# An RWKV channel mix between attention and MLP: another reckoning for the planned order, x loaded by pairs, one activation table, an earlier weight load

## The chip, the cores and the metric

The kernel runs on one core of a Trainium2 chip. The metric is the device time of one execution in microseconds (us); lower is better. TensorE is written PE, its weight loads PEld, VectorE DVE, ScalarE ACT, GpSimd POOL; SP is the engine that issues nearly all DMAs.

## The reference

```python
def _attn_ref(u, v, z):                      # u, v: (4, 3072, 256); z: (4, 3072, 64)
    scores = np.matmul(z, z.transpose(0, 2, 1)) / S
    attn = np.maximum(scores, 0.0) ** 2
    return u * np.matmul(attn, v)

def _moe_ref(x, mu_k, mu_r, w_k, w_v, w_r):  # w_k: (256, 1024), w_v: (1024, 256), w_r: (256, 256)
    x_prev = np.concatenate([np.zeros((B, 1, D)), x[:, :-1, :]], axis=1)
    xk = mu_k * x + (1.0 - mu_k) * x_prev
    xr = mu_r * x + (1.0 - mu_r) * x_prev
    k = np.maximum(xk @ w_k, 0.0)
    v = k * k @ w_v
    return v / (1.0 + np.exp(-(xr @ w_r)))

def _moe2_ref(x, w_in, w_out):               # w_in: (256, 2048), w_out: (2048, 256)
    h = np.maximum(x @ w_in, 0.0)
    return (h * h) @ w_out
```

The three run one after the other; the third takes all 4 x 3072 = 12288 rows of the second as one batch. The weights come as float64.

## The kernel before

Matmuls are done in a float32 form of reduced precision, on operands split into a high part (a cast) and a low part (what is left, a subtraction on DVE). A product is the sum of three matmuls of 128x128 by 128x512: high by high, low by high, high by low. A block is 512 of the 12288 rows; there are 24 blocks, and two make a pair.

*Attention* (function `attention`, from line 261) runs over blocks and, in each, over 24 chunks of keys. Steps that aren't part of the product (loads of z, u and v, transposes, conversion of weights from 64-bit form) hang on numbered steps. At its very start SP and ACT each issue halves of the first two loads of z (`load_z`), seven warm-up matmuls run (L584), and PE transposes z (`prep_z`, L292). Its result u * o is stored transposed to DRAM as xT (L478), and loaded from there by the mix as x (`load_x`, L174).

*The mix* has one pair without and eleven with a Strassen-like scheme (function `mix_groups`, line 989 on). The first pair is plain: two gates (12 matmuls each), 16 hidden tiles (6 matmuls each, `plain_hidden`) and their down products (6 each, `plain_down`, lines 236 to 241). A hidden tile takes a relu (L1080) and a square (L1083) on ACT, a cast (L90) on ACT or DVE, and the rest (L1091) on DVE. After that come groups (s, i): pair s, four groups i each, with seven products (`product`, L850), eight down products (L866 to L868), sums of banks on DVE (`add`, L882), relu, square, cast and rest (L887, L891, L90, L899), and the gates (`gate_unit`, `gate_out`, L637). The sums of w_k that this scheme needs are made at the beginning (`load_wk`, `wk_sums`, L659). Beside all this the next pair is prepared: x is scaled on ACT (`scale_x`, L183) and blended on DVE (`blend`, L192), once for the keys, into a tile of the pair `x2`, and once for the gate. Before, `x` has a tile of one block, so a pair's blocks are loaded in turn: the odd one, the even one, and the odd one again for the gate. Nine pieces of MLP weights are converted from 64-bit form (`conversion`, L132 to L156), and four pieces are split for the MLP (`piece_nodes`).

*The order of the mix* is planned when the program is built. Each step is a node with its engine ("P", "V", "S", "D" for a load, "SV" for a cast that ACT or DVE may do), a cost in us, what it depends on and a due time. PE's order is as written. Due times go back from PE's: each node is due when the node that needs it is due, less cost and 0.2. Then a list scheduler runs from time zero: it takes the engine that can start first, and on it the ready node that is due first. The resulting order is written into the engines' queues; each engine then works through its queue in order, waiting for semaphores. The planned times themselves set nothing else. Before, each load costs 3.5 us, and is taken to start when the plan says so:

```python
            def load(f, *a, deps=()):
                return node("D", 3.5, lambda e: f(*a), *deps)
...
            free = {"P": 0.0, "V": 1.0, "S": 1.0, "D": 0.0}
...
                    i = min((i for i, t in cand.items() if t <= start), key=lambda i: (nodes[i][4], i))
```

Small rings of tiles (`held_by`: "a", "t", "h" and three "raw" tiles for loads of 512 KB) are given out by the planner too.

*The MLP* (line 1408 on, order written by hand) has twelve pairs with eight groups each, of the same seven and eight products, with w_in and w_out split piece by piece; the first piece that isn't split during the mix, number 4, is loaded by `second_pools` (L834), which is called behind the mix. In the group after the first, ACT casts that piece (L647).

A load issued by SP or ACT stands in that engine's queue in program order; when it waits for a semaphore, what stands behind it on the queue waits too. A table for ACT's functions is loaded where the program needs one (ACT_TABLE_LOAD): before the first copy (L297) and before the first sigmoid (L637).

## Time and profile before

| | |
|---|---|
| median of the runs of before | 2473.99 us (2473.72 to 2474.18) |
| the profiled execution | 2473.61 us |
| its span | 2471.7 us |
| PE busy | 2456.2 us (99%) |
| PEld busy | 2028.0 us (82%) |
| DVE busy | 2105.1 us (85%) |
| ACT busy | 1815.6 us (73%) |

Attention takes from 0 to 918.7 us of the span, the mix to about 1492, the MLP the rest. The time of the profiled execution and its span differ by 1.9 us, which lie outside of the span. Matmuls overlap, and their ends are modelled; a busy PE of 99% therefore doesn't say that no time is lost there. In the rows further down, idle time ahead of an instruction and what ended it stand in square brackets, and "xN" merges N instructions in a row.

### The profile page before, as it was taken

How to read it: one execution, taken by the hardware profiler on the slowest of the kernel's cores; microseconds unless marked ns; L12 is line 12 of the kernel's file. 1: busy time of each engine (PE TensorE's matmuls, PEld its weight loads, DVE VectorE, ACT ScalarE, POOL GpSimd, SP SyncE). 2: the span in 40 equal slices, each digit the busy share in tenths (PEclk: the TensorE clock that was granted, in tenths of full speed). 3: DMA queues.
4: the chain of work that ended last, by engine and by line, in shares of the span. 5: the costliest groups of instructions: out<-in, count | busy, mean ns of one | idle time of the engine just before them, and what ended most of it. 6: DMA issues, size and time to landing. Idle time of an engine off the chain costs nothing.

```text
span 2471.7 us, 39362 instructions
## 1 busy us (share of the span) xinstructions
PE 2456.2 (99%) x14721; PEld 2028.0 (82%) x14721; DVE 2105.1 (85%) x3520; ACT 1815.6 (73%) x3216; POOL 0.7 (0%) x6
## 2 busy tenths in 40 slices
PE   9999999999999999999999999999999999999999
PEld 7888898888888887888888887888888888888887
DVE  8898999889899979999999898777777777777776
ACT  8867977888688657888887877666666666666665
POOL 0000000000000000000000000000000000000000
PEclk9999999999999999999999999999999999999999
DMA  7677767776866752222211111110011001100100
GB/s 209 188 227 188 206 200 191 212 207 185 228 194 188 209 154 88 94 86 82 69 52 69 54 67 52 35 33 20 18 35 35 18 18 35 35 18 18 35 18 18
DMA packets 309439, 252.16 MB, mean 102 GB/s; under 512 B 205312, under 2 KB 224768, under 8 KB 306176
## 3 DMA queue, kind: packets, MB, share of 16 engines
q1 hardware_dynamic: 307136, 249.13, 34.5%
q8 instruction: 115, 1.88, 0.3%
q10 hardware_dynamic: 2112, 0.52, 0.1%
q14 instruction: 76, 0.62, 0.1%
HBM read 143.69 MB, written 105.91 MB: 101 GB/s over the span
## 4 chain that ended last, share of the span: by engine, by line
PE 86%; DVE 6%; ACT 4%; issue 2%; DMA 1%; DVEq 0%; SPq 0%
PE v L459 27%; PE ups L850 25%; PE v L868 9%; PE v L866 9%; PE v L867 9%; PE sps L421 4%; PE ups L219 2%; ACT a L382 1%; ACT a L425 1%; DVE st L882 1%; DMA x<-xT 1%; DVE hlo L899 1%; DVE alo L435 0%; DVE turn L362 0%; ACT vhl L328 0%
## 5 line engine op out<-in xcount | busy, mean ns | idle before, releaser
L459 PE MATMUL v<-ahi,vhl 64*128 64x512 f32 x4592 | 668.6, 387 | 0.0
L459 PEld LDWEIGHTS v<-ahi,vhl 64*128 64x128 f32 x4592 | 468.5, 184 | 87.5 <-ACT rest L469 3.9
L887 ACT ACTIVATE s<-s 128x512 f32<-128x512 f32 x288 | 181.0, 628 | 319.9 <-DVE s L882 319.9
L459 PE MATMUL v<-alo,vhl 64*128 64x512 f32 x2296 | 410.7, 386 | 0.1
L866 PE MATMUL v<-hhi,wout 128*128 128x512 f32 x768 | 298.9, 389 | 0.6 <-ACT hhi L90 0.6
L868 PE MATMUL v<-hlo,wout 128*128 128x512 f32 x768 | 298.9, 389 | 0.0
L867 PE MATMUL v<-hhi,wout 128*128 128x512 f32 x768 | 298.8, 389 | 0.0
L850 PE MATMUL ups<-d,win 128*128 128x512 f32 x1056 | 296.5, 389 | 0.0
L459 PEld LDWEIGHTS v<-alo,vhl 64*128 64x128 f32 x2296 | 251.4, 184 | 42.7 <-DVE alo L435 0.6
L899 DVE TENSOR_TENSOR hlo<-s,hhi 128x512 fp32r<-128x512 f32 x384 | 264.3, 688 | 18.1 <-ACT hhi L90 2.8
L891 ACT ACTIVATE s<-s 128x512 f32<-128x512 f32 x384 | 231.4, 628 | 6.1
L882 DVE TENSOR_TENSOR s<-ups,su 128x512 f32<-128x512 f32 x192 | 131.3, 684 | 122.0 <-PE ups L850 121.8
L850 PEld LDWEIGHTS ups<-d,win 128*128 128x128 f32 x1056 | 198.2, 188 | 41.2
L850 PE MATMUL ups<-b,win 128*128 128x512 f32 x792 | 222.4, 389 | 0.0
L435 DVE TENSOR_TENSOR alo<-a,ahi 128x512 fp32r<-128x512 f32 x334 | 219.3, 660 | 0.0
L425 ACT ACTIVATE a<-a 128x512 f32<-128x512 f32 x334 | 211.4, 633 | 10.3
L362 DVE STREAM_TRANSPOSE turn<-a 128x512 f32<-128x512 f32 x240 | 206.5, 860 | 13.9 <-ACT a L425 12.3
L382 ACT ACTIVATE a<-sps 128x512 f32<-128x512 f32 x335 | 197.5, 590 | 19.7 <-PE sps L421 17.1
L850 PEld LDWEIGHTS ups<-b,win 128*128 128x128 f32 x792 | 148.7, 188 | 30.9
L866 PEld LDWEIGHTS v<-hhi,wout 128*128 128x128 f32 x768 | 144.1, 188 | 31.6 <-ACT hhi L90 1.0
L868 PEld LDWEIGHTS v<-hlo,wout 128*128 128x128 f32 x768 | 144.1, 188 | 30.4 <-DVE hlo L899 0.4
L867 PEld LDWEIGHTS v<-hhi,wout 128*128 128x128 f32 x768 | 144.1, 188 | 29.5
(199 smaller groups left out, 4265.4 us busy)
## 6 DMA issues: line engine op xcount, KB each, us to landing
turned<-turn SPq DMA_DIRECT2D x60, 1024.0 KB, 5.0
mixed<-turned SPq DMA_DIRECT2D x220, 256.0 KB, 5.1
x<-xT SPq DMA_DIRECT2D x31, 513.0 KB, 3.8
u<-in_u_dram SPq DMA_DIRECT2D x192, 64.0 KB, 3.6
xT<-uT SPq DMA_DIRECT2D x48, 256.0 KB, 2.4
x2d<-sig SPq DMA_DIRECT2D x48, 256.0 KB, 2.0
x<-x2d SPq DMA_DIRECT2D x12, 1024.0 KB, 4.7
out_dram<-y SPq DMA_DIRECT2D x94, 128.0 KB, 2.3
```

Of the source, the lines that this page charges most:

```text
L362: nc.vector.transpose(t[:, :, :, c, :], a.rearrange("x (m r q) -> x q m r" if s else "x (m q r) -> x q m r", m=G, q=R))
L382: nc.scalar.activation(out=a, in_=ps, func=AF.Relu, scale=1.0 / S)
L425: nc.scalar.activation(out=a, in_=a, func=AF.Square)
L435: finish(lambda: nc.vector.tensor_tensor(out=lo, in0=a, in1=hi, op=ALU.subtract))
L459: nc.tensor.matmul(acc[n, d][i], lhsT=vt[rows, k % 2, c, ds_], rhs=at[s][k // 2][rows], start=first and k == 0, stop=last and k == 2)
L850: nc.tensor.matmul(ps, lhsT=weight(g, h, w), rhs=ops[g[0], j][y], start=first and m == 0, stop=m == 2, skip_group_check=not first)
L866: nc.tensor.matmul(acc[p, b][d], lhsT=w[:, 0, c, ds_], rhs=hi, start=first, stop=False)
L867: nc.tensor.matmul(acc[p, b][d], lhsT=w[:, 1, c, ds_], rhs=hi, start=False, stop=False)
L868: nc.tensor.matmul(acc[p, b][d], lhsT=w[:, 0, c, ds_], rhs=lo, start=False, stop=last)
L887: nc.scalar.activation(out=tmp[g, c], in_=banks[g, 0] if c == "11" else tmp[g, c], func=AF.Relu, scale=1.0 if g[0] < NPAIR else HS)
L891: nc.scalar.activation(out=tmp[g, c], in_=tmp[g, c], func=AF.Square)
L899: nc.vector.tensor_tensor(out=lo, in0=tmp.pop((g, c)), in1=hi, op=ALU.subtract)
```

## The change

- A sigmoid of one column on ACT stands ahead of the first loads of z, into a place that is written again later.
- x of a pair is loaded at once (`load_pair`), into the pair's tile `x2`, which gets eight more columns ahead of each of its two channel halves; the last of them holds the row before the pair. Scaling (`before_x`) reads it shifted by one, and the blend (`blend_x`) is done in place; the first half's blend also waits for the second half's scaling. The load waits until the operands of the pair before are made. The gate's x is still loaded by blocks, after the gate operand before it.
- Loads cost 4.5 (a pair's 5.5) in the plan; the conversions and the sums of w_k can't be planned before `late`, 12 us, plus 1.0.
- In the plan's head, three hidden tiles come before the first gate on PE.
- The costs in the plan are multiplied by a margin (1.05 on DVE, 1.06 on ACT), DVE and ACT are free from 4.0, PE's lag is 0.2, and a cast that ACT may do too counts as due 9 us later when DVE chooses.
- Piece 4 is loaded by a node of the plan, after the last conversion and the last piece before it, into the third raw tile; `second_pools` no longer loads it.

```diff
@@ -573,6 +573,7 @@
                 for i in range(ND * (2 - n)):
                     at_step(s - 1 + 12 * n + 2 * i, mix, n, i // ND, i % ND)
             ones = nc.const_aps.tensor(1.0, [P, T], BF16)
+            nc.scalar.activation(out=om[:, 0, 0:1], in_=ones[:, 0:1], func=AF.Sigmoid)
             load_z(0, 0, (nc.sync, nc.scalar))
             nc.sync.dma_start(out=v_first, in_=v[0, 0:T, :].rearrange("(c p) d -> p c d", p=P))
             load_z(0, 1, (nc.scalar, nc.sync))
@@ -715,19 +716,38 @@
 
     unit = {}
 
-    def staged_x(s, b, c):
-        if s not in x2_raw:
-            x2_raw[s] = hp.tile([P, ND, 2 * T], F32, tag="x2", name="x2")
-        return x2_raw[s][:, c, b * T:(b + 1) * T]
-
-    def stage_x(s, b, c, m=None):
-        blend(2 * s + b, 0, c, staged_x(s, b, c), m)
+    HALO = 8
+
+    def pair_tile(s):
+        x2_raw[s] = hp.tile([P, ND, HALO + 2 * T], F32, tag="x2", name="x2")
+        return x2_raw[s]
+
+    def pair_x(s):
+        return x2_raw[s][:, :, HALO:].rearrange("x c (b t) -> x c b t", b=2)
+
+    def load_pair(s):
+        b, t0 = 2 * s // NB, 2 * s % NB * T
+        t = pair_tile(s)
+        src = xT[b].rearrange("(c p) s -> p c s", p=P)
+        if t0:
+            nc.sync.dma_start(out=t[:, :, HALO - 1:], in_=src[:, :, t0 - 1:t0 + 2 * T])
+        else:
+            nc.vector.memset(t[:, :, HALO - 1:HALO], 0.0)
+            nc.sync.dma_start(out=t[:, :, HALO:], in_=src[:, :, 0:2 * T])
+
+    def before_x(s, b, c, m):
+        t0 = HALO - 1 + b * T
+        nc.scalar.activation(out=m, in_=x2_raw[s][:, c, t0:t0 + T], func=AF.Copy, scale=om[:, 0, c:c + 1])
+
+    def blend_x(s, b, c, m):
+        x = pair_x(s)[:, c, b]
+        nc.vector.scalar_tensor_tensor(out=x, in0=x, scalar=mu[:, 0, c:c + 1], in1=m, op0=ALU.mult, op1=ALU.add)
...
     def op_src(s, j):
-        src = x2_raw[s].rearrange("x c (b t) -> x c b t", b=2)
+        src = pair_x(s)
         if j in (2, 3):
             return x2_tmp[s][:, j - 2]
         return src[:, *{0: (0, 0), 1: (0, 1), 4: (1, 0), 5: (1, 1), 6: (1, 0)}[j]]
@@ -802,11 +822,11 @@
         next(splits[i])
 
     def load_x2(s):
-        x2_raw[s] = t = hp.tile([P, ND, 2 * T], F32, tag="x2", name="x2")
-        nc.sync.dma_start(out=t, in_=x2d[s - NPAIR].rearrange("(c p) t -> p c t", p=P))
+        t = pair_tile(s)
+        nc.sync.dma_start(out=t[:, :, HALO:], in_=x2d[s - NPAIR].rearrange("(c p) t -> p c t", p=P))
 
     def prep_x2(s, k):
-        src = x2_raw[s].rearrange("x c (b t) -> x c b t", b=2)
+        src = pair_x(s)
         b11, b12, b21, b22 = src[:, 0, 0], src[:, 0, 1], src[:, 1, 0], src[:, 1, 1]
         if k == 0:
             x2_tmp[s] = t = hp.tile([P, 2, T], F32, tag="d13", name="d13")
@@ -817,11 +837,13 @@
             nc.vector.tensor_tensor(out=b21, in0=b21, in1=b12, op=ALU.subtract)
         else:
...
             return halves(t[:, 0], t[:, 1], x)
 
@@ -831,7 +853,6 @@
         pools["ops", 1] = ctx.enter_context(tc.tile_pool(name="ops1", bufs=1, side="right", reuse_waits="tile"))
         for q in range(2, 4):
             w_tiles(w4, q)
-        load_piece(4)
 
     def mlp():
         gt, acc = {}, {}
@@ -1018,8 +1039,8 @@
             def on_pe(f, *a, deps=(), cost=0.68):
                 return node("P", cost, lambda e: f(*a), *deps)
 
-            def load(f, *a, deps=()):
-                return node("D", 3.5, lambda e: f(*a), *deps)
+            def load(f, *a, deps=(), cost=4.5):
+                return node("D", cost, lambda e: f(*a), *deps)
 
             def get(*k):
                 return last.get(k)
@@ -1030,18 +1051,15 @@
                 last["op", s, j] = on_v(op_lo, s, j, deps=(hi,))
                 return last["op", s, j]
 
-            def blended(n, which, c, *deps):
-                place = (lambda: raw_r(n, c)) if which else (lambda: staged_x(n // 2, n % 2, c))
-                m = on_s(lambda: scale_x(n, which, c, place()), deps=(*deps, get("x", n)), cost=0.63)
-                if which:
-                    take(m, "t", ("xr", n, c))
-                f = (lambda: blend_r(n, c, place())) if which else (lambda: stage_x(n // 2, n % 2, c, place()))
-                return on_v(f, deps=(m,), cost=0.63)
+            def gate_blend(n, c, *deps):
+                m = on_s(lambda: scale_x(n, 1, c, raw_r(n, c)), deps=(*deps, get("x", n)), cost=0.63)
+                take(m, "t", ("xr", n, c))
+                return on_v(lambda: blend_r(n, c, raw_r(n, c)), deps=(m,), cost=0.665)
 
             def gate_operand(n, *deps):
                 done = []
                 for c in range(ND):
-                    xm = use(blended(n, 1, c, *deps), ("xr", n, c))
+                    xm = use(gate_blend(n, c, *deps), ("xr", n, c))
                     hi = use(either(r_hi, n, c, deps=(xm,)), ("xr", n, c))
                     last["xr", n, c] = use(on_v(r_lo, n, c, deps=(hi,)), ("xr", n, c))
                     done.append(xm)
@@ -1108,13 +1126,19 @@
                     cast(on_act, hi, xr1[c])
 
             def prepare(s, clear):
-                m0 = 2 * s
-                last["x", m0 + 1] = load(load_x, m0 + 1, deps=last["xr done"])
-                b1 = [blended(m0 + 1, 0, c, *clear) for c in range(ND)]
-                last["x", m0] = load(load_x, m0, deps=b1)
-                b0 = [blended(m0, 0, c, *clear) for c in range(ND)]
-                last["staged", s] = [*b0, *b1]
-                last["b0"] = b0
+                ready = load(load_pair, s, deps=clear, cost=5.5)
+                done, m_of = [], {}
+                for b in (1, 0):
+                    for c in range(ND):
+                        def scaled(b=b, c=c):
+                            m_of[b, c] = place.pop(("m", s, b, c))
+                            before_x(s, b, c, m_of[b, c])
+                        m = take(on_s(scaled, deps=(ready,), cost=0.63), "t", ("m", s, b, c))
+                        f = lambda b=b, c=c: blend_x(s, b, c, m_of[b, c])
+                        done.append((b, c, m, f))
+                m1 = {c: m for b, c, m, f in done if b}
+                xs = [use(on_v(f, deps=(m, None if b else m1[c]), cost=0.665), ("m", s, b, c)) for b, c, m, f in done]
+                last["staged", s] = xs
                 head(s)
 
             def head(s):
@@ -1124,16 +1148,19 @@
                 operand(s, 1, on_v(sums, s, 1, deps=(last["tops"],)))
 
             def gate_part(s, r_free):
-                xs = gate_operand(2 * s, *r_free)
-                last["x", 2 * s + 1] = load(load_x, 2 * s + 1, deps=(*xs, *last["b0"]))
+                last["x", 2 * s] = load(load_x, 2 * s, deps=last["xr done"])
+                last["x", 2 * s + 1] = load(load_x, 2 * s + 1, deps=gate_operand(2 * s, *r_free))
 
             def tail(s):
                 for j in range(2, 6):
                     operand(s, j, last["tops"])
                 operand(s, 6, on_v(sums, s, 2, deps=(last["op", s, 4], last["op", s, 1])))
 
+            late = node("D", 12.0, lambda e: None)
+
             def wk_nodes(h, *deps):
                 total = use(take(load(load_wk, h, deps=(get("wk"),)), "raw", ("wk32", h)), ("wk32", h))
+                total = node("D", 1.0, lambda e: None, total, late)
                 for k in range(2):
                     total = use(on_v(wk_sums, h, k, deps=(total,), cost=0.7), ("wk32", h))
                     if k == 0:
@@ -1146,6 +1173,7 @@
             def conversion(i, src, put, due):
                 key = "w", i
                 i = use(take(load(load_raw, key, src, src.shape[1], src.shape[2], deps=(last.get("conv"),)), "raw", key), key)
+                i = node("D", 1.0, lambda e: None, i, late)
                 steps = convert(key, put, 0)
                 for k, f in enumerate(steps):
                     i = on_v(f, deps=(i,), cost=0.6 if k in (3, 6, 7) else 0.335, due=due)
@@ -1186,6 +1214,8 @@
                 use(on_pe(down1, n, f, False, cost=0.91, deps=(hi,)), ("h", n, f))
                 return use(on_pe(down1, n, f, True, cost=0.45, deps=(lo,)), ("h", n, f))
 
+            for k in order1[:lead]:
+                plain_hidden(*k)
             plain_gate(0)
             for c in range(ND):
                 m = take(on_s(plain_m, c, deps=(last["r", 0],), cost=0.63), "a", ("xr1", c))
@@ -1195,8 +1225,6 @@
                 for i in (xm, hi, last["xr", 1, c]):
                     use(i, ("xr1", c))
                 last.setdefault("xr done", []).append(xm)
-            for k in order1[:lead]:
-                plain_hidden(*k)
             prepare(PLAIN, ())
             for i, (n, f) in enumerate(order1):
                 if i + lead < len(order1):
@@ -1333,8 +1361,12 @@
                     piece_nodes(PIECE_PAIRS.index(s), 49.0 + 46.2 * s)
                 before = g
 
+            take(load(load_piece, 4, deps=(last["piece"], last["conv"])), "raw", ("w32", 4))
+
             n = len(nodes)
-            LAG = {"P": 0.3, "V": 0.15, "S": 0.15, "D": 0.0}
+            MARGIN = {"P": 1.0, "V": 1.05, "S": 1.06, "D": 1.0}
+            BEHIND_CASTS = 9.0
+            LAG = {"P": 0.2, "V": 0.15, "S": 0.15, "D": 0.0}
 
             def cost_on(i, e):
                 c = nodes[i][1]
@@ -1348,7 +1380,7 @@
             for i in reversed(range(n)):
                 for d in nodes[i][3]:
                     nodes[d][4] = min(nodes[d][4], nodes[i][4] - cost_on(i, nodes[i][0][0]) * (nodes[i][0] != "P") - 0.2)
-            free = {"P": 0.0, "V": 1.0, "S": 1.0, "D": 0.0}
+            free = {"P": 0.0, "V": 4.0, "S": 4.0, "D": 0.0}
             users, missing = [[] for _ in nodes], [len(x[3]) for x in nodes]
             for i, x in enumerate(nodes):
                 for d in x[3]:
@@ -1361,7 +1393,7 @@
                 t = ready[i]
                 for ring, key in takes.get(i, ()):
                     free_at = [(max([ended[k] + 0.15 for k in users_of[x]], default=0.0), q) for q, x in enumerate(held_by[ring])
-                               if all(k in ended for k in users_of[x])]
+                               if all(k in ended for k in users_of[x]) and (key != ("w32", 4) or q == 2)]
                     if not free_at:
                         return None
                     t, chosen[i] = max(t, min(free_at)[0]), (ring, min(free_at)[1], key)
@@ -1377,7 +1409,7 @@
                     if not cand:
                         continue
                     start = max(free[e], min(cand.values()))
-                    i = min((i for i, t in cand.items() if t <= start), key=lambda i: (nodes[i][4], i))
+                    i = min((i for i, t in cand.items() if t <= start), key=lambda i: (nodes[i][4] + BEHIND_CASTS * (e + nodes[i][0] == "VSV"), i))
                     if best is None or start < best[0]:
                         best = start, e, i
                 start, e, i = best
@@ -1385,8 +1417,9 @@
                     pe.pop(0)
                 else:
                     waiting.remove(i)
-                free[e] = start + (cost_on(i, e) if e != "D" else 0.1)
-                ended[i] = end = start + cost_on(i, e)
+                took = cost_on(i, e) * MARGIN[e]
+                free[e] = start + (took if e != "D" else 0.1)
+                ended[i] = end = start + took
                 if i in takes:
                     ring, q, key = chosen[i]
                     held_by[ring][q] = key
```

## Rows read from the trace of the kernel before

**Rows 1.** Stretches: length, busy (count) of PE, PEld, DVE, ACT, POOL, PEclk, DMA share, GB/s.
```profile
918.70:1492.00 573.30, 568.34 (x2495) 468.40 (x2494) 536.13 (x929) 470.02 (x829) 0.00 (x0) 1.00 0.22 74
...
1510.00:2465.00 955.00, 955.00 (x4215) 790.51 (x4214) 725.63 (x1167) 633.54 (x1130) 0.00 (x0) 1.00 0.08 24
```

**Rows 2.** Instructions in order of time, 912 to 945 us: start, duration, engine, line, operation.
```profile
921.39 5.40 PEld L219 LDWEIGHTS ups<-mixed,wk 128*128 128x128 f32 x24
...
922.68 0.45 SPq L103 DMA_DIRECT2D raw<-in_moe_w_out_dram  x1
...
926.88 0.43 DVE L132 TENSOR_SCALAR sa<-raw 128x512 uint32<-128x512 uint32 x1 [4.62 <-DMA raw<-in_moe_w_out_dram]
928.15 0.89 DVE L659 TENSOR_TENSOR raw<-raw 128x256 f32<-128x256 f32 x2 [0.84 <-DMA raw<-w_k]
...
930.06 0.62 ACT L90 CAST mixed<-sa 128x512 fp32r<-128x512 f32 x1 [5.28 <-DVE sa L192]
...
931.25 0.29 PEld L240 LDWEIGHTS v<-hhi,wv 128*128 128x128 f32 x1 [4.46 <-ACT hhi L90]
...
935.33 0.19 PEld L240 LDWEIGHTS v<-hhi,wv 128*128 128x128 f32 x1
```

**Rows 3.** Stretches as in rows 1, after the wait at 931 us.
```profile
931.20:934.00 2.80, 2.74 (x7) 2.08 (x8) 2.80 (x6) 2.19 (x6) 0.00 (x0) 0.50 0.55 170
```

**Rows 4.** Waits of PEld, 1488 to 1520 us: total, times, longest.
```profile
PEld v L866 <- ACT hhi L90: 1.0, 1, 1.0
PEld ups L850 <- ACT s L887: 0.7, 1, 0.7
PEld v L868 <- DVE hlo L899: 0.4, 1, 0.4
PEld ups L850 <- DVE sv L882: 0.2, 1, 0.2
```

**Rows 5.** Instructions in order of time, 1484 to 1512 us: ACT at the MLP's first cast.
```profile
1497.91 1.02 ACT L647 CAST win<-raw 128x256 fp32r<-128x256 f32 x3 [5.93 <-DMA raw<-w_in]
```

**Rows 6.** Waits of PEld, 936 to 1488 us.
```profile
PEld ups L850 <- DVE sa L882: 2.1, 4, 1.1
PEld ups L850 <- ACT sig L637: 0.8, 2, 0.6
```

**Rows 7.** A stretch of the mix, columns as in rows 1.
```profile
1100.00:1150.00 50.00, 50.00 (x222) 41.33 (x221) 49.59 (x87) 42.81 (x76) 0.00 (x0) 1.00 0.25 85
```

**Rows 8.** Waits of DVE, 918 to 1490 us, the longest in total.
```profile
DVE x L192 <- ACT x L183: 14.9, 12, 1.7
```

**Rows 9.** Groups by line and form: the casts of hidden tiles by either engine.
```profile
L90 DVE CAST hhi<-st 128x512 fp32r<-128x512 f32 x70 | 29.3, 420 | 3.9 <-ACT st L891 3.6
...
L90 ACT CAST hhi<-st 128x512 fp32r<-128x512 f32 x106 | 65.3, 620 | 2.2
```

**Rows 10.** Instructions in order of time, 0 to 20 us.
```profile
0.73 1.10 ACTq L281 DMA_DIRECT2D zn<-in_z_dram  x2
...
0.77 2.72 PE L584 MATMUL sps<-const-bfloat16-1.0 128*128 128x512 bf16 x6 [0.77 <-PEq L1514]
...
1.86 1.28 ACT L297 ACT_TABLE_LOAD   x1 [1.86 <-issue]
...
3.51 0.71 PEld L292 LDWEIGHTS zps<-unit,zn 128*128 128x128 f32 x4 [0.93 <-issue]
```

**Rows 11.** DMA issues of ACT at 0.73 and 1.28 us: KB each, us to landing.
```profile
zn<-in_z_dram ACTq DMA_DIRECT2D x1, 128.0 KB, 2.7
...
zn<-in_z_dram ACTq DMA_DIRECT2D x1, 128.0 KB, 4.7
```

**Rows 12.** Chain of waits, 0 to 60 us: shares by line.
```profile
by line: DVE turn L362 12.8%; DVE alo L435 12.7%; PE v L459 9.6%; issue 9.1%; ACT a L425 7.2%; ACT a L382 6.8%; PE sps L421 5.7%; PE v L453 4.6%; DVE vhl L326 4.6%; PE sps L584 4.5%; DVE ahi L428 4.5%; PE sps L392 3.5%; PE zps L292 3.2%; AC
```

**Rows 13.** ACT's sequencer at the last store (L917): durations in ns, first and last start.
```profile
L917 ACTq EVENT_SEMAPHORE  x1: 17/17/17, 2465.8 to 2465.8; - x1
```

**Rows 14.** Instructions in order of time, 2462 to 2472 us: the last two evictions.
```profile
2465.77 0.66 ACT L906 ACTIVATE ys<-v 128x256 f32<-128x256 f32 x2 [0.76 <-PE v L868]
```

6 lines of the change are left out of this document (4 added, 2 removed).

## The prediction, made before the changed kernel was run

> **What bounds the kernel now.** I read first the busy time of each engine in long stretches. From 1510 us on, 4215 matmuls take 955.00 us and TensorE never goes short: 0.2266 us for each, which I use as the step of a matmul throughout [rows 1]. That stretch can't be shortened by an order of other engines. In the stretch from 918.7 to 1492 us (the mix, whose order the kernel plans itself) TensorE is not quite full, and VectorE is at 536 of 573 us [rows 1]. So the question is how much time TensorE loses, and where. The busy time of PE doesn't tell that, since the modelled end of a matmul (0.39 us) reaches over the next start. I therefore count the starts of the weight loads (PEld), one for each matmul: where a start comes later than the last one plus 0.2266, time is lost. I find three places.
>
> The first is the opening of the mix. 24 weight loads start at 921.39, so the next one is due at 921.39 + 24 x 0.2266 = 926.83. It comes at 931.25, after 4.46 us of idle time put down to a cast on ScalarE. Twelve matmuls later the next such group should start at 926.83 + 12 x 0.2266 = 929.55 and starts at 935.33 [rows 2]. The loss is 935.33 - 929.55 = 5.78 us: 4.42 of waiting, and 1.36 since the matmuls behind the wait run slowly. The granted clock is 0.50 from 931.2 to 934, the lower of the two levels, after TensorE stood still for four microseconds [rows 3].
>
> Why the cast was late is in the same rows. ScalarE's queue had another cast in front, which waited 5.28 us for VectorE's blend. VectorE in turn sat in front of two steps whose operands were still on their way: the first conversion step, which started at 926.88 after 4.62 us of waiting for a load issued at 922.68, and the weight sums at 928.15 [rows 2]. The planner reckons a load as landed after 3.5 us, counted from a time at which SP hasn't issued it yet.
>
> The second place is the end of the mix. Four waits of PEld between 1488 and 1520 us make 1.0 + 0.7 + 0.4 + 0.2 = 2.3 us [rows 4]. A PEld is idle 0.04 us in any case (0.2266 less the 0.188 of a load), so 2.1 us are lost. The reason: ScalarE waits 5.93 us for the first weight piece of the MLP [rows 5].
>
> The third is scattered. From 936 to 1488 us PEld waits four times for sums on VectorE (2.1 us) and twice for the sigmoid on ScalarE (0.8) [rows 6], less 6 x 0.04: 2.7 us. VectorE is the reason there: 49.59 of 50 us between 1100 and 1150 [rows 7], although 14.9 us of its time goes into waiting for the scaled x, twelve times [rows 8].
>
> All that can be won behind the attention is 5.8 + 2.1 + 2.7 = 10.6 us.
>
> **The change part by part.** *Later and longer loads.* The planner now holds the first conversion and the weight sums back until 12 us after its zero, lets VectorE and ScalarE start at 4, and puts the first three hidden tiles on TensorE before the gate. On TensorE these are the same 36 matmuls in another order, then the first down product. The first hidden tile is thus done after 6 matmuls (1.4 us) and not after 18 (4.1 us), and its relu, square, cast and rest take four steps of 0.4 to 0.7 us, so some 3 us with the hand-overs. They are ready near 923 us, four before the first down product asks for them. VectorE no longer has the loads in front: planned zero lies at about 918.7, so 12 us is 930.7, and the two loads of before had landed by 926.9 and 928.2 [rows 2]. The new loads on SP are queued behind the same stores of xT, one of them of 1 MB, so all three (2 MB) should be there by 930 to 931.5. What the plan may still have wrong is the pair's load, which it takes as landed 5.5 us after zero, while SP issues it only near 923. ScalarE would then stand in front of the scaling of x, and behind it are queued the relu and square of hidden tile 3 or 4. TensorE asks for these only at 926.83 + 3 x 2.72 = 935, and for the bank of tile 3 at about 936.4. That cover is some 4 us; without it, each microsecond of delay is a microsecond of the end. I take the whole 5.8 us as won; the bounds are 4.4 (the clock falls for a shorter wait all the same) and 5.8.
>
> *The margins, and casts after other work on VectorE.* A cast costs VectorE 0.42 us and ScalarE 0.62 [rows 9], and 70 of the hidden ones lie on VectorE. If half of all such casts go over, VectorE gets 35 x 0.42 = 15 us free and ScalarE 35 x 0.62 = 22 us more: 470 + 22 = 492 of 573 us [rows 1], still less full than VectorE. With the pair's x loaded early, a part of the 14.9 us goes too. So I expect the scattered waits to shrink. But a wait here depends on the order in a single group of 11.5 us, and new ones may come. I take half, 1.4 us, between -1 (new waits) and 2.7.
>
> *One load of x for a pair.* Scalings and blends stay the same in number and shape. A pair's three loads of 513 KB become one of 1 MB and two of 513 KB. The DMA share of this stretch is 0.22 [rows 1], so the 11 x 0.5 MB more are hidden. The load has to wait for the last operands of the pair before, as it fills their buffer. On SP it has the gate's x, the next conversion's raw load and the stores of x2d behind it. All these have a group or more of 11.5 us of lead, and no PE wait of before is put down to a transfer there. Blending in place puts the blend of the first half behind the scaling of the second, one step of 0.7 us in a lead of some 30. I cost both at nothing.
>
> *The first weight piece early.* The load moves from behind the mix to the time after the last conversion, on a raw tile that no one needs by then. ScalarE doesn't wait at 1492, and all four waits behind it go: 2.1 us. The load of the next piece keeps its place and is used only 12 us later. The lower bound is 1.5, as the casts of the piece still have to be done there.
>
> *One activation table.* The load of a table at the start of the mix takes 1.28 us and goes; it doesn't count again, since the path there went through VectorE. What counts is the beginning. A sigmoid of one column is now the first instruction of ScalarE, and the two loads of z that ScalarE issues stand behind it. Before, the issue starts at 0.73, the table is loaded behind it at 1.86, and the warm-up matmuls end at 3.49; the transposes of z start at 3.51, as the half issued by ScalarE has landed after 2.7 us, at 3.43 [rows 10, 11]. There is no slack. If the issue waits for the table, it moves by 1.28 + about 0.15 = 1.4 us, and then competes with the first load of v, as did the second z load, which took 4.7 us [rows 11]: the delay is 1.4 to 3.4 us, and the chain carries all of it, as in the first 60 us it goes through the work of the engines, and none of the steps that it names there is a transfer [rows 12].
>
> Does it wait? At the end of the kernel ScalarE has a load's semaphore instruction behind two half evictions. It runs at 2465.8, when the first of the two has just started (2465.77) and the second not at all [rows 13, 14]. So what ScalarE's sequencer handles itself doesn't wait for the work queued before it, and issuing a DMA is of that kind. I take 0 for the beginning, with 3.4 as the other end.
>
> [...]
>
> **The sum.** 5.8 + 1.4 + 2.1 + 0 = 9.3 us off the profiled execution's 2473.61: 2464.3. The median of the runs is 0.4 above that execution, so 2464.7.
>
> **The rivals.** *The issue waits for the table.* For it: a table load might hold the sequencer as no other instruction does, and the trace shows none with an issue behind it. Against it: rows 13. It costs 1.4 to 3.4, I take 2.2: 2466.9. If TensorE's clock also stays at the lower level, as it stood still between warm-up and transposes, another microsecond.
>
> *The opening's wait changes its place.* The pair's load is later than planned, and ScalarE stands before it so long that TensorE waits for hidden tile 3 or 4. For it: the plan's 5.5 us is short. Against: 4 us of cover. If 4 us remain and the clock's 1.4 with them, the gain is 9.3 - 5.4 = 3.9: about 2470. The same time comes out if the new order does little for the mix and only the weight piece and a part of the opening are won.
>
> *Slower: ScalarE becomes the bound.* Casts are sent to ScalarE whenever VectorE has more urgent work. If all 70 hidden casts go over, ScalarE has 470 + 70 x 0.62 = 513 of 573 us, and the groups that also scale x (four of 0.7 us) exceed their 11.5 us. A relu that frees a bank is then late by a cast of 0.62. This decides once it happens in more than 13 of the 44 groups (8 us, what opening and piece bring). In 22 groups with the late issue on top: 2464.7 + 1.4 + 13.6 + 2.2 = 2481.9. Against it: ScalarE waits for others in most groups now.
>
> **How the numbers follow.** My forecast has 0.54, the late issue 0.27, the moved wait 0.13, the slower case 0.06. A measurement of this kernel can tell about 0.2%, 5 us, from no change. The forecast and the late issue lie below 2469.0, save a small part of the latter; the moved wait lies at the border or inside. So faster 0.79, same 0.15, slower 0.06. The range takes in everything won (2473.61 - 10.6 + 0.4 = 2463.4, and 0.3 for a wait on a bank at the first matmul of the mix) and the late issue at its worst with nothing won of the scattered waits (2473.99 - 7.9 + 3.4 = 2469.5): 2463.1 to 2469.5.
>
> **What would show it.** Right: weight loads without a wait over 1 us between 921 and 940 us and a granted clock of 1.00 there; ScalarE at the end of the mix with no wait for the weight piece; fewer waits for sums on VectorE; the ACTq issue still at 0.7 to 0.9 us beside a running table load. Wrong: an issue at 2.1 us and transposes near 5; a wait for a transfer of x in ScalarE's queue with TensorE idle behind it; TensorE waits for ScalarE all over the mix. The forecast falls if the opening's 5.8 us don't go, as no other part brings half as much.

## The result: 0.85% slower, and the profile after

| | before, run beside it | after |
|---|---|---|
| median | 2474.06 us (2473.67 to 2474.45) | 2495.21 us (2494.05 to 2495.92) |
| ratio | | 1.0085, interval 1.0072 to 1.0098 |
| span of the profiled execution | 2471.7 us | 2493.6 us |

I had forecast 2464.7 us. Every wait that the prediction wanted to remove is gone, and still the kernel is 21 us slower. First the opening of the mix, where the 5.78 us were lost [rows 2, 3]. Columns as there; after, in order of time:

```profile
919.25 3.98 PEld L219 LDWEIGHTS ups<-mixed,wk 128*128 128x128 f32 x18 [0.35 <-ACT rest L469]
...
923.26 2.68 PEld L219 LDWEIGHTS ups<-mixed,wr 128*128 128x128 f32 x12
...
925.99 1.32 PEld L219 LDWEIGHTS ups<-mixed,wk 128*128 128x128 f32 x6
...
927.35 0.19 PEld L240 LDWEIGHTS v<-hhi,wv 128*128 128x128 f32 x1
...
929.65 0.73 ACT L740 ACTIVATE st<-x,om 128x512 f32<-128x512 f32 x1 [0.16 <-DMA x<-xT]
...
932.24 0.42 DVE L132 TENSOR_SCALAR sa<-raw 128x512 uint32<-128x512 uint32 x1
```

The first down product (L240) comes 36 weight loads after 919.25, thus is due at 919.25 + 36 x 0.2266 = 927.41; it comes at 927.35, and the granted clock is 1.00 from 921 to 940 us. No wait is left. VectorE's first conversion step (L132), which had stood 4.62 us in front of everything [rows 2], now runs at 932.24 without a wait; ScalarE waits 0.16 us for the pair's x.

The end of the mix [rows 5], ScalarE at the first cast of the MLP's weights, after:

```profile
1495.02 1.02 ACT L648 CAST win<-raw 128x256 fp32r<-128x256 f32 x3
```

No wait stands there, and PEld has no wait at all between 936 and 1520 us, where it had those of rows 4 and 6. Now the stretches [rows 1, 7] (length, busy time and count of PE, PEld, DVE, ACT, POOL, granted clock, DMA share, GB/s), after:

```profile
918.70:1492.00 573.30, 573.30 (x2485) 465.65 (x2482) 530.89 (x902) 474.27 (x850) 0.00 (x0) 1.00 0.24 85
1100.00:1150.00 50.00, 50.00 (x218) 40.63 (x217) 47.29 (x80) 42.99 (x79) 0.00 (x0) 1.00 0.26 90
1510.00:2465.00 955.00, 955.00 (x4127) 774.54 (x4126) 714.14 (x1145) 621.04 (x1108) 0.00 (x0) 1.00 0.08 24
```

Here is the loss. From 1510 us on, a part whose order of work the change doesn't touch, 4127 matmuls run where 4215 did: 955 / 4127 = 0.2314 us each in place of 0.2266, on a TensorE that is always busy, waits for nothing and has its full granted clock. Between 1100 and 1150 there are 218 in place of 222. The chain of waits and the list of waits say nothing of this; the count in a stretch of fixed length does (and with the count the busy time of PEld falls, from 790.51 to 774.54 us).

More closely, by the start of a bank's eviction that comes once in each group of 45 matmuls: before, a group in the MLP takes 10.20 us, that is 45 x 0.2267. After, it takes 10.46, that is 45 x 0.2324; in every second MLP pair the last three groups fall back to 10.34, 10.20, 10.20. MLP pairs take 83.48 and 83.13 in turn (before 81.60), and 43 groups of the mix 508.5 us (before 499.3).

What differs in groups whose instructions are the same? The addresses. In the built program, bytes past a multiple of 256 at which the tiles start in each partition ("operand tiles" are the moving operands of the products):

```
                                          before   after
h (hidden tiles), wk, wv, wr                0        0
w_in, w_out, quarters 0 and 1               0       64
w_in, w_out, quarters 2 and 3               0        0
operand tiles of the mix                    0       64
operand tiles of the MLP, one pair of two   0       64
operand tiles of the MLP, the other         0        0
```

The pair's tile `x2` has eight more columns in two halves, 2 x 8 x 4 = 64 bytes, and all that is allocated behind it on that side moves by 64. The groups at 10.20 are those in which every operand has 0. So have the matmuls of the opening (the blended x, wk, wr, wv and the hidden tiles), which is why the old step still fits there.

### The profile page after: what moved, and what is told of

It is laid out like the page before. It is cut to its first block, busy times and chain, and to the rows that moved or that the text cites. A ratio compares the mean times of both kernels' runs of the same rounds, so it can differ in the third digit from the quotient of the medians.

```text
span 2493.6 us, 39375 instructions
## 1 busy us (share of the span) xinstructions
PE 2483.6 (100%) x14721; PEld 2057.5 (83%) x14721; DVE 2104.8 (84%) x3499; ACT 1823.0 (73%) x3240; POOL 0.7 (0%) x6
## 4 chain that ended last, share of the span: by engine, by line
PE 94%; ACT 3%; DVE 1%; issue 1%; DMA 0%; SPq 0%; DVEq 0%
PE v L459 27%; PE ups L871 27%; PE v L887 10%; PE v L889 10%; PE v L888 10%; PE sps L421 4%; PE ups L219 4%; ACT a L382 1%; ACT a L425 1%; DVE alo L435 0%; DVE turn L362 0%; ACT vhl L328 0%; DMA mixed<-turned 0%; PE v L240 0%; PE v L238 0%
## 5 line engine op out<-in xcount | busy, mean ns | idle before, releaser
L459 PE MATMUL v<-ahi,vhl 64*128 64x512 f32 x4592 | 675.8, 387 | 0.0
L459 PEld LDWEIGHTS v<-ahi,vhl 64*128 64x128 f32 x4592 | 487.8, 184 | 69.6 <-ACT rest L469 3.7
L459 PE MATMUL v<-alo,vhl 64*128 64x512 f32 x2296 | 418.0, 386 | 0.2 <-DVE alo L435 0.2
L887 PE MATMUL v<-hhi,wout 128*128 128x512 f32 x768 | 303.2, 395 | 0.0
L888 PE MATMUL v<-hhi,wout 128*128 128x512 f32 x768 | 301.6, 393 | 0.0
L459 PEld LDWEIGHTS v<-alo,vhl 64*128 64x128 f32 x2296 | 261.7, 184 | 34.0 <-DVE alo L435 0.6
```

Source lines behind the costliest of these rows:

```text
L459: nc.tensor.matmul(acc[n, d][i], lhsT=vt[rows, k % 2, c, ds_], rhs=at[s][k // 2][rows], start=first and k == 0, stop=last and k == 2)
L887: nc.tensor.matmul(acc[p, b][d], lhsT=w[:, 0, c, ds_], rhs=hi, start=first, stop=False)
L888: nc.tensor.matmul(acc[p, b][d], lhsT=w[:, 1, c, ds_], rhs=hi, start=False, stop=False)
```

## Experiments

The letters in the expectations: A is the theory that the addresses of TensorE's operands set its step (first in the form that a multiple of 128 bytes is enough), B that addresses don't matter and the loss lies in something else, C that they matter only beside other engines' traffic, D that the distance between the two operands counts.

### The changed kernel with other displacements

Only the halo's width, or a pad, is changed; order and instructions stay. (e2, e3, e4, e7, e8, e9 and e13 were executed once each.)

```diff
-    HALO = 8
+    HALO = 16     # e1_halo16: operands displaced by 128 bytes
+    HALO = 64     # e5_halo64: by 512
+    HALO = 32     # e6_halo32: by 256
# e2_pad_behind_hp, HALO = 8: the tiles behind x2 in its pool stay at 64, matmul operands go to 128
+        ctx.enter_context(tc.tile_pool(name="odd", bufs=1)).tile([P, 16], F32, name="odd")
         w3 = ctx.enter_context(tc.tile_pool(name="w3", bufs=1, reuse_waits="tile"))
```

> The changed kernel with 16 columns ahead of each half of the pair's tile instead of 8. Everything that lies behind this tile in a partition then starts 128 bytes further on than before the change, not 64. Theory A (addresses): the matmul step of 0.2324 us that the changed kernel shows in mix and MLP comes from operands that start 64 bytes past a multiple of 128; here the step is 0.2267 as before, the opening, the end and the scattered waits of the mix stay gone, and the time is 2474.1 - 10.6 = 2463.5, between 2462.5 and 2465. Theory B (order): the new order of the queues makes TensorE's step longer; it is kept here, and the time stays near 2495.

Measured 2491.52 us (2490.42 to 2492.93; 1.0069 of before, 1.0052 to 1.0086), a group 10.43 us. A miss: 128 bytes aren't enough.

> The changed kernel with an unused tile of 64 bytes behind the pool that holds the pair's tile. The operands of the matmuls (operand tiles, weights of the MLP) start at multiples of 128 again, while the pair's x, the sigmoid's tiles and the differences, which only VectorE and ScalarE touch, stay 64 bytes past one. Theory A in its first form (the matmuls' own operands decide): 2463 to 2465, step 0.2267. Theory A in its second form (VectorE and ScalarE work on displaced tiles and disturb TensorE's reads): near 2495. Theory B (order): near 2495.

Measured 2491.47, a group 10.43 again: a miss too. Whether the tiles that only VectorE and ScalarE use lie at 64 (here) or at 128 (e1) makes no difference.

> The changed kernel with 64 columns ahead of each half of the pair's tile: everything behind it starts 512 bytes further on than before the change (the changed kernel: 64; the run with 16 columns: 128, which was as slow). Theory A now says that the displacement against the other tiles decides, and that 64 and 128 bytes are both wrong; at 512 each operand has the position of before to a multiple of 512, the step is 0.2267, a group of the MLP takes 10.20 us and the time is 2463.5, between 2462.5 and 2465. Theory B (order): 2491 to 2495.

> The same with 32 columns, a displacement of 256 bytes. Before the change every operand of a matmul started at a multiple of 256, and each at 256 past a multiple of 512. If a multiple of 256 is what counts: 2462.5 to 2465, groups of 10.20 us. If the position to a multiple of 512 counts: slow, between 2480 and 2492, as the steps at 64 and 128 bytes gave groups of 10.46 and 10.43. Theory B: 2491 to 2495.

Measured 2464.07 us (2463.64 to 2465.11) with 64 columns, 0.9959 of the kernel before (0.9945 to 0.9973), and 2464.25 (2462.61 to 2465.76), 0.9961 (0.9946 to 0.9976), with 32. A group takes 10.20 and an MLP pair 81.6 us again. The stretch from 1600 to 2000 us with 16, then with 32 columns:

```profile
1600.00:2000.00 400.00, 400.00 (x1736) 326.19 (x1735) 298.29 (x478) 261.99 (x466) 0.00 (x0) 1.00 0.09 26
```

```profile
1600.00:2000.00 400.00, 400.00 (x1767) 331.15 (x1766) 304.41 (x487) 265.94 (x475) 0.00 (x0) 1.00 0.09 27
```

These two versions beat both kernels. The displacement had cost 2495.2 - 2464.2 = 31 us, and the rest of the change wins 10, about what I had forecast (2464.7).

### The kernel before, with displaced operands

If addresses do it, the old kernel must become slow by a pad alone.

```diff
 # e3_before_all64: weights of quarters 0, 1 and operand tiles of that side at 64
+        ctx.enter_context(tc.tile_pool(name="odd", bufs=1)).tile([P, 16], F32, name="odd")
         w3 = ctx.enter_context(tc.tile_pool(name="w3", bufs=1, reuse_waits="tile"))
 # e4_before_weights64, both pads: weights at 64, operand tiles at 128 (e8_before_weights64: 112 for the second 16, operand tiles at 512)
+        ctx.enter_context(tc.tile_pool(name="odd2", bufs=1)).tile([P, 16], F32, name="odd2")
 # e7_before_moving64, a pad of 16 behind w3 alone: weights at 0, operand tiles at 64
         units = ctx.enter_context(ExitStack())
```

> The kernel before with an unused tile of 64 bytes ahead of the MLP's first weights, and nothing else: its order is the old one, and operand tiles and the weights of MLP quarters 0 and 1 start 64 bytes past a multiple of 128. Theory A: the step is 0.2324 in the mix's groups and in most of the MLP; about 44 groups x 50 matmuls and 84 of 96 groups x 45, 6000 matmuls x 0.0057 = 34 us more, less the 3 to 4 us of waits that a slower TensorE covers: 2503 to 2508. Theory B (order): no change, 2474.

Measured 2503.78 us, where the executions of before beside it take 2472.6 to 2476.8: B falls, and A's number comes. The mix's groups take 508.5 us and the MLP pairs 83.13 and 83.48, as in the changed kernel to the hundredth. One pad without a single instruction changed gives the same slow groups; the kernel loses 28 us by it.

> The kernel before with 64 unused bytes ahead of the MLP's weights of quarters 0 and 1, and 64 more behind them: only these weights are displaced, all moving operands start at multiples of 128. If displaced weights are enough, the groups of the MLP that use quarters 0 and 1 (four to four and a half of eight) take 10.46 instead of 10.20 us: 12 x 4.25 x 0.26 = 13 us more, 2486 to 2489, and the mix keeps its step. If only the moving operand counts, 2474. Theory B: 2474.

Measured 2500.48, a miss for the same reason as e1: 128 isn't harmless.

> The kernel before with 64 unused bytes ahead of the operand tiles alone (the tiles of the mix's products, and in the MLP those of the even pairs); all weights stay where they were. If a displaced moving operand is enough: the mix's groups and the six even pairs of the MLP are slow, the odd pairs are not (81.6 us): 8.5 + 6 x 1.9 = 20 us more, 2492 to 2496. If only weights count: 2474. Theory B: 2474.

> The kernel before with 64 unused bytes ahead of the MLP's weights of quarters 0 and 1 and 448 behind them: only these weights are displaced by 64, and the operand tiles by 512. (In the run with 64 and 64, the operand tiles were displaced by 128, so that it didn't tell the two apart.) If displaced weights are enough and 512 is harmless: the mix as before, four to five of eight groups in each MLP pair at 10.4 to 10.5 instead of 10.20 us, 12 x 4.5 x 0.26 = 14 us more, 2485 to 2490. If only moving operands count: 2474. If 512 is not harmless: 2500 and more. Theory B: 2474.

Measured 2497.27 (1.3 above the range) and 2489.72. In each, the slow groups are those whose operands are displaced: with only the weights displaced the mix, which doesn't use them, keeps its 499.3 us; with only the operand tiles displaced it takes 508.0, and of the MLP pairs one in two stays fast. Two neighbouring pairs of e7_before_moving64:

```profile
1740.00:1820.00 80.00, 80.00 (x354) 66.20 (x353) 60.17 (x97) 52.23 (x94) 0.00 (x0) 1.00 0.08 25
1825.00:1905.00 80.00, 80.00 (x346) 64.60 (x345) 58.53 (x94) 51.71 (x92) 0.00 (x0) 1.00 0.06 14
```

In the slow pair the down products, whose operands all lie at 0, run at a long step too: 0.2321 us on average from the start of one of their weight loads to the next load, 0.2331 for the up products (before: 0.2263 and 0.2270). That fits no rule of A's kind that takes each matmul by itself.

### TensorE alone

> Computes nothing of the reference: stretches of 240 matmuls (128x128 by 128x512) on constant operands that start at a multiple of 256 bytes or so many bytes past one; in the second half VectorE and ScalarE work beside them on tiles of their own. Theory A (the addresses alone set the step): 0.2266 us with nothing displaced and with 256 bytes, 0.2324 with the moving operand, the weights or both 64 past, 0.2318 with 128 past, a mean of 0.2295 where displaced and undisplaced sixes take turns, or 0.2324 if one displaced matmul slows its neighbours as in the MLP, and the same with the other engines at work. Rival C (TensorE's reads collide with those of VectorE and ScalarE when the addresses differ): 0.2266 everywhere in the first half, 0.2324 only for the displaced stretches of the second.

A stretch is a loop of 240 matmuls over slices of one moving and one weight tile:

```diff
+        return dict(lhsT=wt[:, b:b + P], rhs=mv[:, a:a + T], start=k == 0, stop=k == 5)
...
+    for i in range(N):
+        nc.tensor.matmul(bank(i), **one(i, 16, 0))    # moving operand 16 x 4 bytes past
```

Weight loads in order of time, one line for each stretch of the first half (displacement in bytes of moving operand and weights, from the source: L70 0, 0; L72 64, 0; L74 0, 64; L76 64, 64; L78 128, 0; L80 32, 0; L82 256, 0; L84 moving 64 and 0 in turns of six):

```profile
23.23 54.36 PEld L70 LDWEIGHTS w<-mv,wt 128*128 128x128 f32 x240
77.62 54.91 PEld L72 LDWEIGHTS w<-mv,wt 128*128 128x128 f32 x240
132.57 55.95 PEld L74 LDWEIGHTS w<-mv,wt 128*128 128x128 f32 x240
188.56 54.39 PEld L76 LDWEIGHTS w<-mv,wt 128*128 128x128 f32 x240
242.99 55.71 PEld L78 LDWEIGHTS w<-mv,wt 128*128 128x128 f32 x240
298.75 55.95 PEld L80 LDWEIGHTS w<-mv,wt 128*128 128x128 f32 x240
354.75 54.39 PEld L82 LDWEIGHTS w<-mv,wt 128*128 128x128 f32 x240
409.18 55.40 PEld L84 LDWEIGHTS w<-mv,wt 128*128 128x128 f32 x240
```

From start to start and by 240: 0.2266, 0.2290, 0.2333, 0.2268, 0.2323, 0.2333, 0.2268, 0.2310 us. The other engines stand still here, and beside 640 instructions of VectorE and 460 of ScalarE the same stretches take the same time (0.2267, 0.2289, 0.2333): C falls. The granted clock is 1.00 from 135 to 185 us, in the first half; from 30 to 950 us, of which TensorE is busy for 732, it is 0.90 on average. The surprise is the fourth line. With both operands displaced by 64 bytes nothing is lost. So A in its simple form falls too, and D comes up: it isn't either address, it is how far one lies from the other modulo 256.

> Computes nothing of the reference: again stretches of 240 matmuls on constant operands, with TensorE alone. Theory D (what counts is how far the weights lie from the moving operand modulo 256 bytes, not either address): weights 224 past behave as the moving operand 32 past did (0.2333 us), 192 as the moving operand 64 past (0.2290), 128 as 128 (0.2323), weights and moving operand both 32 or both 192 past as nothing displaced (0.2267). Theory A (each operand has to start at a multiple of 256): every displaced stretch above 0.2285, the ones displaced alike too. Where displaced and undisplaced matmuls take turns, D for the operands of one matmul gives 0.2267 when both take turns together, and the mean, 0.2278, when only the moving one does; if the weights loaded beside the matmul before are what counts, taking turns together gives 0.2300 and weights that follow the moving operand of the matmul before 0.2267.

Step of each stretch, from the starts of the weight loads as above:

```
weights past the moving operand (bytes)   0      32     64     96     128    160    192    224
step (us)                               0.2267 0.2333 0.2333 0.2343 0.2324 0.2333 0.2290 0.2333
both 32 past 0.2268; both 192 past 0.2269
turns of six: both together 0.2305, weights alone 0.2321, moving alone 0.2310
turns of three: moving alone 0.2327
turns of one: both together 0.2317, weights the other way round 0.2316, weights alone 0.2300, moving alone 0.2309
```

(The 64 of the first row and the six of the moving operand are from the run before.) Three of its rows: weights 32 past; both 32 past; and a stretch whose moving operand lies at 0 in the first half and at 64 in the second:

```profile
77.77 55.95 PEld L72 LDWEIGHTS w<-mv,wt 128*128 128x128 f32 x240
...
412.71 54.40 PEld L84 LDWEIGHTS w<-mv,wt 128*128 128x128 f32 x240
...
910.27 54.69 PEld L102 LDWEIGHTS w<-mv,wt 128*128 128x128 f32 x240
```

D's numbers for fixed distances come out as expected: weights 224 past like moving 32 past, 192 like 64, 128 like 128, and equal displacement costs nothing. Its numbers for turns don't: when both operands take turns together the distance is always 0, yet the step is 0.2305 to 0.2317, and the variant for weights loaded beside the matmul before fails too. So taking turns can cost as well. It doesn't in every pattern: six of the eight lie 0.0021 to 0.0050 above the mean of their distances, but weights alone in turns of one come out at it (0.2300, the mean of 0.2267 and 0.2333), and the other way round nearly so (0.2316 against 0.2312). A single change half way costs nothing to speak of: 54.69 us, where the two halves alone make 54.64. With turns of three, as in the kernel's interleaved up and down products, the step is 0.2327, close to the 0.2324 of the slow groups. That fits the undisplaced matmuls that were slow beside displaced ones.

> The kernel before, with 64 bytes more at either end of the pools, so that every tile from which TensorE reads starts 64 past a multiple of 256 bytes, weights and moving operands alike. Theory D (the distance between the two counts): 2474 to 2476 us, 0.2267 us per matmul in the MLP, 1766 in the 400 us from 1600 on. Theory A (each operand has to start at a multiple of 256): all 6710 matmuls of mix and MLP slow, 6710 x 5.8 ns = 39 us, so 2513 at least, 1730 matmuls in that stretch.

```diff
-    xp.tile([P, 8], F32, name="even")
+    xp.tile([P, 24], F32, name="even")
-    ctx.enter_context(tc.tile_pool(name="edge", bufs=1, side="right")).tile([P, 56], F32, name="even")
+    ctx.enter_context(tc.tile_pool(name="edge", bufs=1, side="right")).tile([P, 40], F32, name="even")
```

The same long stretch, every operand of a matmul 64 past a multiple of 256:

```profile
1510.00:2465.00 955.00, 955.00 (x4215) 790.76 (x4214) 726.30 (x1169) 633.80 (x1131) 0.00 (x0) 1.00 0.09 24
```

4215 matmuls, as many as in rows 1. The time is 2476.86 us (2475.24 to 2479.88; 1.0011 of before, 1.0000 to 1.0023), 0.9 above D's range and 36 below A's; mix and MLP are as before (499.7, 81.6), and what little is added lies outside of them (the mix's first weight load comes 1.4 us later, and the way from the MLP's last group to the end takes 1.0 more). A falls in the kernel too: operands have to lie alike, not on a multiple of 256. As nothing takes turns in this run either, it doesn't tell how much of the 31 us comes from the distance within a matmul and how much from the turns; that stays open.

### What the parts are worth with the operands aligned

All three are e6_halo32 with one part undone.

```diff
 # e10_piece_late
-            take(load(load_piece, 4, deps=(last["piece"], last["conv"])), "raw", ("w32", 4))
+        load_piece(4)          # in second_pools, as before
 # e11_no_table
-            nc.scalar.activation(out=om[:, 0, 0:1], in_=ones[:, 0:1], func=AF.Sigmoid)
 # e12_old_reckoning
-            def load(f, *a, deps=(), cost=4.5):
+            def load(f, *a, deps=(), cost=3.5):
-                ready = load(load_pair, s, deps=clear, cost=5.5)
+                ready = load(load_pair, s, deps=clear, cost=3.5)
-            late = node("D", 12.0, lambda e: None)
+            late = node("D", 0.0, lambda e: None)
...
-            BEHIND_CASTS = 9.0
+            BEHIND_CASTS = 0.0
```

(In e12 the two nodes of 1.0 behind `late`, the margins, the lag and the engines' starts also go back to the old values.)

> The changed kernel with 32 columns ahead (all matmul operands at multiples of 256 bytes) and with the first MLP piece loaded behind the mix as before. The prediction's term: 2.1 us (1.5 at least) on top of the 2464.25 us of the kernel with the early load, so 2465.8 to 2466.4, with ScalarE waiting some 5.9 us for the piece near 1490 us and the four waits of TensorE back there. Rival: the new order leaves ScalarE so far ahead that the wait is hidden: 2464.3, no wait of TensorE.

Measured 2465.07 us (2464.98 to 2465.81), below the range. The mix is unchanged (498.1 us); the first MLP pair takes 82.48 in place of 80.95, so the early piece is worth 1.5 us in the trace, the lower end of its range. The medians differ by 0.8 only, but the mix begins anywhere between 917.9 and 920.3 us in these four kernels, which share one attention, so they can't tell more. The wait is back, and so are the four behind it. ScalarE in order of time, then the waits of PEld (total, times, longest):

```profile
1489.68 1.02 ACT L648 CAST win<-raw 128x256 fp32r<-128x256 f32 x3 [5.70 <-DMA raw<-w_in]
```

```profile
PEld v L888 <- ACT hhi L90: 1.0, 1, 1.0
PEld ups L872 <- ACT s L909: 0.4, 1, 0.4
PEld v L890 <- DVE hlo L921: 0.4, 1, 0.4
...
PEld ups L872 <- DVE sv L904: 0.2, 1, 0.2
```

> The changed kernel with 32 columns ahead, without the sigmoid at the very beginning. The prediction's term: 0, so 2464.3 (2463.8 to 2464.8); two table loads, the second of 1.28 us near 922 with no wait of TensorE behind it, the first issue at 0.73 and the transposes of z at 3.51 and not 3.60. Rival: the second table load delays the first gate's sigmoid and TensorE behind it, 1.3 us: 2465.6. Other rival: the table at the start costs what the late issue would, so that without it the time falls by 1.4 to 3.4: 2461 to 2463.

Measured 2464.20 us (2463.78 to 2464.53): no difference. The second table load is there, hidden, and the transposes of z start at 3.60 without the sigmoid, not at 3.51; with it they start at 3.60 (after) and 3.74 (32 columns). Without it:

```profile
3.60 0.71 PEld L292 LDWEIGHTS zps<-unit,zn 128*128 128x128 f32 x4 [1.02 <-issue]
...
924.60 1.28 ACT L637 ACT_TABLE_LOAD   x1
```

> The changed kernel with 32 columns ahead, with the plan reckoning as before: loads of 3.5 us, no later start of the conversions and sums of w_k, no margins, VectorE and ScalarE free from 1.0, TensorE's lag 0.3, no preference for casts. The pair's load, the hidden tiles ahead of the gate, the early piece and the table stay. The prediction's theory: the opening's stall comes back, 4.4 to 5.8 us, and 1.2 us or so of scattered waits: 2469.9 to 2471.3, TensorE waiting over 4 us between 921 and 940. Rival: three hidden tiles ahead of the gate are what wins the opening, since hidden tile 0 is then done early: 2464.3 to 2465.5 and no wait over 1 us there.

Measured 2474.88 us (2474.01 to 2477.16), ratio to before 1.0000 (0.9990 to 1.0009). The whole gain is gone, 10.6 us, and not the 5.6 to 7.0 of my expectation. Where it goes can be counted by the starts of weight loads. From the first of the mix to the first of a product 45.73 us pass in place of 43.45 (in the kernel before 49.23): of the opening's 5.8 us, 2.3 come back. From there to the MLP's first product it takes 517.4 us in place of 508.6 (before 511.0): 8.7 us, in waits all over the mix. Instructions in order of time, then waits of PEld:

```profile
930.81 0.72 ACT L740 ACTIVATE st<-x,om 128x512 f32<-128x512 f32 x1 [6.20 <-DMA x<-xT]
...
932.06 1.23 PEld L219 LDWEIGHTS ups<-mixed,wk 128*128 128x128 f32 x6 [2.38 <-ACT sa L1098]
```

```profile
PEld ups L871 <- DVE st L903: 3.0, 8, 0.6
PEld ups L219 <- ACT sa L1098: 2.4, 1, 2.4
PEld ups L871 <- ACT sa L1098: 2.1, 1, 2.1
PEld v L889 <- DVE hlo L920: 1.9, 6, 0.6
```

In the opening ScalarE stands 6.2 us in front of the pair's x, which lands at 930.8, and the relu that frees a bank is queued behind it. This is the rival of the moved wait, in a kernel that plans the pair's load at 3.5 us: the wait for a conversion's load became a shorter one for x. So both sides of my expectation miss. The opening keeps 3.5 of its 5.8 us without the new reckoning. The larger part of the loss is scattered, and there the parts that stayed in (the pair's load, the hidden tiles ahead, the early piece) are 6.4 us worse with the old reckoning than the kernel before was. e12 takes back the loads' cost, the later start, the margins and the casts all at once; which of them the gain needs, it doesn't show.

## Why the prediction was wrong, point by point

*What bounds the kernel.* The three places were read rightly, and all three are gone. The sentence on the stretch from 1510 us, "That stretch can't be shortened by an order of other engines", is right but was used for more: I took 0.2266 us as a fixed step of a matmul. It depends on how the operands lie (0.2267 to 0.2343 us in e13). Every sign that the prediction named for being right came (no wait and a full clock in the opening, no wait for the weight piece, no waits for sums, the issue at 0.80 us), and the time was wrong all the same: none of these signs looks at the step.

*One load of x for a pair: the step that failed.* "I cost both at nothing" looked at the DMA share, the queue and the blend's dependency, and passed over what the diff says plainly, that the pair's tile grows by eight columns in each half. That moves everything behind it by 64 bytes, and the price is 31 us. No row of the trace before has a displaced matmul, so the price couldn't be read there. But the part got neither a price nor a bound for this, and the step of a matmul was taken as given. Nor was the rest of the part free in every order: with the plan's old reckoning the mix behind its opening is 6.4 us slower than before (e12), though there other parts stayed in with it. There was a sign in the code: two tiles named `even` ([P, 8] and [P, 56]) that nothing reads or writes. Their only effect can be on addresses.

*Later and longer loads.* Predicted 5.8 (4.4 to 5.8), and no wait is left in the opening: with 32 columns 43.45 us pass to the first product in place of 49.23, which is 5.78. By e12, 2.3 of them need the new reckoning; the other 3.5 come with the hidden tiles ahead or the pair's load, which no run takes apart. The lower end of the range let the clock fall for a shorter wait too; around e12's wait of 2.38 us the granted clock is 1.00 (900 to 940 us).

*Margins and casts.* Predicted 1.4 of the 2.7 us. PEld has no wait there any more, and from the first product of the mix to the MLP's first 508.64 us pass with 32 columns in place of 510.99: 2.35 came. That it was the margins and the casts isn't shown, as no run undoes them alone. Casts of hidden tiles on VectorE went from 70 [rows 9] to 40.

*Early piece.* Predicted 2.1, at least 1.5; 1.5 in e10.

*One table.* Predicted 0, with 3.4 as the other end; 0 in e11. The row that decides it, after:

```profile
0.73 1.28 ACT L576 ACT_TABLE_LOAD   x1 [0.73 <-PEq L1547]
...
0.80 1.03 ACTq L281 DMA_DIRECT2D zn<-in_z_dram  x2
...
2.03 0.20 ACT L576 ACTIVATE om<-const-bfloat16-1.0 128x1 f32<-128x1 bf16 x1
```

ScalarE's queue issues the two loads of z at 0.80, beside a table load that runs until 2.01. The inference from rows 13 to this start held. The next ACTIVATE starts at 2.03, 0.02 us after the table load ends; in e11, too, the load at 924.60 ends at 925.88 and the sigmoid behind it starts at 925.90.

*The sum.* With the addresses put right, 5.8 + 2.35 + 1.5 = 9.6 us off; from the mix's first weight load to the kernel's last it is 1552.9 - 1543.4 = 9.5 in the traces of before and e5, and 2474.5 - 2464.1 = 10.4 by the medians of e5 and of before beside it, which have the attention's spread in them. The forecast's 9.3 comes near this partly by luck: the scattered waits brought 0.95 more than forecast and the piece 0.6 less. Its result was wrong for a price that it didn't have.

*The rivals.* The late issue falls by the row above. The moved wait didn't come (0.16 us); with the old reckoning it does, at 2.4 us (e12). ScalarE as the bound falls: 474 us busy in the stretch of rows 1 (480 with 32 columns) against 470, and TensorE doesn't wait for it. The case that came, slower with no wait anywhere, was none of them: all my rivals were waits.

## What to carry to other kernels

An edit that changes the size of a tile can move what is allocated behind it (here by 64 bytes, at 31 us), so compare the addresses of matmul operands modulo 256 in the two programs before costing it at nothing, and keep weights and moving operands of all interleaved matmuls alike (from 1510 us on 0.2266 us a matmul with all at 0 or, in e14, all at 64; 0.2314 in the changed kernel). When a kernel gets slower and no engine waits more, count the instructions of the bound engine in a stretch of fixed length (4127 matmuls in 955 us in place of 4215): it separates a longer step from lost time, which no list of waits does. The times that a plan assumes decide which wait an in-order queue stands in front of: with 3.5 us in the plan for the pair's load, ScalarE stood 6.2 us in front of it (e12), with 5.5 and the rest of the new reckoning 0.16. When a change has several parts, undo them one at a time: e12 took the whole reckoning back at once and can't say which number of it counts.

## What the runs showed of the hardware that I had not expected

- The step of a 128x128 by 128x512 matmul of this float32 form, each with its own weight load, at a granted clock of 1.00, depends on where weights and moving operand start: 0.2267 us at distance 0 modulo 256 bytes, 0.2290 at 192, 0.2323 to 0.2343 at 32, 64, 96, 128, 160 and 224. Both displaced alike cost nothing (0.2268, 0.2269).
- Taking turns between addresses can cost of itself, also at distance 0: 0.2305 (turns of six) and 0.2317 (turns of one). Weights alone in turns of one cost nothing beyond their distances (0.2300).
- Work of VectorE and ScalarE beside it doesn't change the steps measured with it (0.2267, 0.2289, 0.2333), nor does it matter whether their own tiles lie at 64 or 128 (2491.47 and 2491.52 us).

What in the chip makes the distance count, and why a change from one matmul to the next costs, stays open: the runs give the step for each pattern and not its cause.
